# Splitting some stores by rows: 128 rows as 2 and 126, 5 rows as 1 and 4 or 2 and 3

## The chip, the cores and the metric

The kernel runs on one core of one Trainium2 chip. The metric is the device time of one execution in microseconds. A core has the engines PE (matrix products), DVE (vector), ACT (scalar), POOL (general) and SP (here it only issues transfers), and 16 DMA engines that all transfers share. A transfer issued by SP goes to one queue (q1 in the profile), a transfer issued by POOL to another (q0); every DMA engine works on both.

## The reference

The kernel computes one decode step of a transformer block and its gradients, in bf16:

```python
x = A_x                                                # (2, 1, 640)
h  = x + attn(layernorm(x), k_cache, v_cache, wq, wo)  # 32 heads, 4096 keys, head size 128
h2 = h + relu(layernorm(h) @ w1) @ w2                  # w1: 640 x 1728
...
return (h2, *vjp(grad_out))     # gradients of x, k_cache, v_cache, wq, wo, w1, w2
```

The caches have 2 x 32 x 4096 x 128 elements each, 67 MB, and so have their gradients. The gradients of the weights are outer products of two rows per batch element: wq 640 x 4096, wo 4096 x 640, w1 640 x 1728, w2 1728 x 640.

## The kernel before

The order of all work is written out by hand: each stage is a Python generator, and a loop at the end of the function takes a step of one, then of another. There are 64 pairs of batch element and head.

**First pass** (`p1_iter`): for each pair, K and V are loaded as [128, 32 x 128] tiles of 1 MB on SP's queue, K is transposed on PE, and scores, softmax and the products that the gradients need are made.

**Second pass** (`p2_iter`): for each pair V is loaded once more (tile Wt, but for a few that are kept), and the gradients gK and gV, 1 MB each, are made on DVE (L954; gV in part on ACT, L1024) and stored, at first on POOL's queue (L1025, L1040), and from the end of the first pass on SP's (L1004, L1025). POOL also makes the small copies pp (L992) that gV needs.

**Beside the second pass** two more generators run. `fin_gen` makes the weight gradients, out_7 (w2), out_6 (w1), out_5 (wo) and out_4 (wq), by calling `outer_rows`. `gx_gen` and `mlp_out` make the gradient of x (out_1) and the output (out_0) and end in `store_row`.

`outer_rows` (L1070) takes the rows of an output in groups. With `cc` rows to a partition and P = nrow / cc partitions (128 in all calls here), partition p holds rows p*cc to p*cc + cc - 1 of the output. For each group it takes a tile `ot` from the pool "f" (a tile comes back no sooner than 13 steps after it was given back), fills it by products on PE (L1093) and copies on ACT (L1099), and stores it with one transfer on POOL's queue (L1101). For out_7 the last 64 rows are stored apart (L1103). There are 18 stores at L1101: three for out_7, three for out_6, six for out_5, six for out_4, most of them of 0.86 to 1.05 MB.

`store_row` (L699) transposes a column of 640 values into 5 rows of 128, copies them on DVE (L705) into one of two halves of a scratch row, and stores them on SP's queue (L706), 1.2 KB. It runs four times.

What sets the order around the change: SP and POOL each issue their transfers strictly in the order of the program, and an issue that waits holds up all that stands behind it on the same engine. SP's transfers take eight semaphores in turn, and POOL's another eight; an issue waits until the transfer that used its semaphore last, eight places before, has landed. It also waits for the engine that filled the tile. A tile that is stored is filled again only when its store has landed.

Of the kernel before, what the change touches and what calls it, by code (L numbers as in the profile page):

```python
# [15 lines left out]
def kernel(  # L16
# [20 lines left out]
    nc = tc.nc  # L37
# [58 lines left out]
    def pst(shape, dtype, role, name):  # L96

        k = banks[role].pop(0)
        banks[role].append(k)
        return ps.tile(shape, dtype, tag=f"bank{k}", bufs=1, name=name)  # L100
# [11 lines left out]
    def take(tag, shape, name):  # L112
        assert free[tag] > 0, (tag, name)
        free[tag] -= 1
        k = homes[tag].pop(0)
        t = pools[k].tile(shape, BF16, tag=tag_of.get(k, f"big{k}"), bufs=1, name=name)
        home_of[id(t)] = (tag, k, t)
        return t
# [9 lines left out]
    def give(t, to=None):  # L128
        tag, k, _ = home_of.pop(id(t))
        to = to or goes_to(tag)  # L130
        owned[tag] -= 1
        owned[to] += 1
        free[to] += 1
        homes[to].append(k)
        given_at[k] = step[0]

    def rested(tag, n):

        return free[tag] > 0 and (forced[0] or step[0] >= given_at.get(homes[tag][0], -n) + n)
# [557 lines left out]
    nrow = [0]  # L697

    def store_row(col_bf, n, dst):  # L699

        t = pst([16, 128], BF16, "mid", "row_ps")
        nc.tensor.transpose(t[0:n, :], col_bf, ident_bf[:])
        r = junk_row[0:16, D - 128 * (1 + nrow[0] % 2):D - 128 * (nrow[0] % 2)]
        nrow[0] += 1
        nc.vector.tensor_copy(out=r[0:n, :], in_=t[0:n, :])  # L705
        nc.sync.dma_start(out=dst, in_=r[0:n, :])  # L706

    def ttr(in0, in1, acc, width, kc=128, junk=None):
        if junk is None:
# [57 lines left out]
    def mlp_out():  # L767

        ml32 = sm("ml32", FP32, ND, B)
        nc.vector.memset(ml32[:], 0.0)  # L770
        for k in range(NW2):
            while free["q"] < 1 or "arow" not in FIN:
                yield 0.0 if "arow" not in FIN else 0.5
            t = load_w2(k, "q", "(p c) d -> p c d")
            yield from wait(12)
            c1 = min(NF, (k + 1) * FP)
            m_ps = pst([128, ND, B], FP32, "mid", "mlp_ps")
            for c in range(ND):
                for cf in range(k * FP, c1):
                    kc = f_kc(cf)  # L780
                    nc.tensor.matmul(m_ps[:, c, :], lhsT=t[0:kc, cf - k * FP, c * 128:(c + 1) * 128],
                                     rhs=arow[0:kc, cf, :], start=(cf == k * FP), stop=(cf == c1 - 1))
            give(t)
            yield
            nc.vector.tensor_tensor(out=ml32[:], in0=m_ps[:], in1=ml32[:], op=ALU.add)
        ml_bf = sm("ml_bf", BF16, ND, B)
        nc.vector.tensor_copy(out=ml_bf[:], in_=ml32[:])
        y_bf = sm("y_bf", BF16, B, ND)
        nc.vector.tensor_tensor(out=y_bf[:].rearrange("p b c -> p c b"), in0=h1c[:], in1=ml_bf[:], op=ALU.add)
        yield from wait(3)  # L790
        for b in range(B):
            store_row(y_bf[:, b, :], ND, out_0[b].rearrange("s (c p) -> (s c) p", p=128))
            yield
# [272 lines left out]

    late = {}
    spreading = [False]

    def outer_rows(L, nrow, R, N, out_ap, cc, rest=0):  # L1070

        P = nrow // cc
        grp = max(1, min(cc, 4096 // N))
        out_v = out_ap[0:nrow, :].rearrange("(p c) n -> p c n", c=cc)
        for c0 in range(0, cc, grp):
            gn = min(grp, cc - c0)
            while not rested("f", 13):
                yield 0.0
            ot = take("f", [128, grp, N], "ot")
            todo = [(k, n0, min(512, N - n0), P, L[:, bass.ds(c0 + k, P, step=cc)])  # L1080
                    for k in range(gn) for n0 in range(0, N, 512)]
            more = rest if c0 + gn == cc else 0
            assert not more or gn < grp
            if more:
                todo += [(gn, n0, min(512, N - n0), more, L[:, nrow:nrow + more]) for n0 in range(0, N, 512)]
            made = []
            for x in range(len(todo) + 1):
                if x < len(todo):
                    k, n0, nn, kp, cols_of = todo[x]
                    q = 32 * (fw[0] % 4)  # L1090
                    o_ps = pst([128, 512], FP32, "o", "o_ps")
                    fw[0] += 1
                    nc.tensor.matmul(o_ps[0:kp, 0:nn], lhsT=cols_of[q:q + B], rhs=R[q:q + B, n0:n0 + nn],  # L1093
                                     start=True, stop=True)
                    made.append((o_ps, k, n0, nn, kp))
                    yield 0.3
                if x > 0:
                    o_ps, k, n0, nn, kp = made[x - 1]
                    nc.scalar.copy(out=ot[0:kp, k, n0:n0 + nn], in_=o_ps[0:kp, 0:nn])  # L1099
                    yield 0.3  # L1100
            nc.gpsimd.dma_start(out=out_v[:, c0:c0 + gn, :], in_=ot[0:P, 0:gn, :])  # L1101
            if more:
                nc.gpsimd.dma_start(out=out_ap[nrow:nrow + more, :], in_=ot[0:more, gn, :])  # L1103
            give(ot)

    def fin_gen(fin):
# [13 lines left out]
        FIN["arow"] = True  # L1120
        yield
        yield from outer_rows(FIN["ar"], NFF * 128, FIN["gr"], D, out_7, NFF, F_rem)
        yield from rows_of(fin, ghfc, NF, "ghfr", "rX")
        yield from rows_of(fin, x2c, ND, "x2r", "rD")
        yield from outer_rows(FIN["x2r"], D, FIN["ghfr"], Dff, out_6, ND)
        HH = H // 2
        while ("gh1", B - 1) not in done:
            yield
        yield from rows_of(fin, gh1c, ND, "gh1r", "rD")
        for s0 in range(0, H, HH):  # L1130
            yield from rows_of(fin, OFc[:, s0:s0 + HH, :], HH, "OFr", "rX")
            yield from outer_rows(FIN["OFr"], HH * 128, FIN["gh1r"], D, out_5[s0 * 128:(s0 + HH) * 128, :], HH)
# [7 lines left out]
    def gx_gen(fin):  # L1140
# [50 lines left out]
        for b in range(B):  # L1191
            gxo = sm(f"gxo{b}", BF16, ND)
            nc.vector.tensor_copy(out=gxo[:], in_=gx_bf[:, :, b])
            yield from wait(2)
            store_row(gxo[:], ND, out_1[b].rearrange("s (c p) -> (s c) p", p=128))
            yield
# [232 lines left out]
```

## Time and profile before

| | us |
|---|---|
| median of 3 runs | 892.6 (890.12 to 892.91) |
| the profiled execution | 887.9 |
| its span, from the first to the last instruction | 886.1 |

| engine | busy us | share of the span |
|---|---|---|
| PE | 736.0 | 83% |
| DVE | 690.8 | 78% |
| ACT | 478.0 | 54% |
| POOL | 155.8 | 18% |

| transfers | count | KB each | us from issue to landing, median |
|---|---|---|---|
| Kt, Vt, Wt loads on SP's queue | 180 | 1024 | 18.7, 15.1, 16.4 |
| gK, gV stores on SP's queue | 101 | 1024 | 16.7, 15.1 |
| gK, gV stores on POOL's queue | 27 | 1024 | 10.3, 10.4 |
| ot stores on POOL's queue (L1101) | 18 | 160 to 1024 | 10.5 |
| row stores on SP's queue (L706) | 4 | 1.2 | not told |

The profile is of one execution, and times in it are counted from the start of its span. "DMA" in its slices and windows is the mean busy share of the 16 DMA engines, so that 1.00 is all sixteen busy, and 0.06 is one of them. The trace also has a record of each packet that a DMA engine moved, with its queue, start, duration and size, but not with the engine's number, and a record of each update of a semaphore. A transfer has landed when its semaphore has risen by 16.

### The profile page before, as it was taken

How to read it: one execution, taken by the hardware profiler on the slowest of the kernel's cores; microseconds unless marked ns; L12 is line 12 of the kernel's file. 1: busy time of each engine (PE TensorE's matmuls, PEld its weight loads, DVE VectorE, ACT ScalarE, POOL GpSimd, SP SyncE). 2: the span in 40 equal slices, each digit the busy share in tenths (PEclk: the TensorE clock that was granted, in tenths of full speed). 3: DMA queues.
4: the chain of work that ended last, by engine and by line, in shares of the span. 5: the costliest groups of instructions: out<-in, count | busy, mean ns of one | idle time of the engine just before them, and what ended most of it. 6: DMA issues, size and time to landing. Idle time of an engine off the chain costs nothing.

```text
span 886.1 us, 24945 instructions
## 1 busy us (share of the span) xinstructions
PE 736.0 (83%) x10215; PEld 614.3 (69%) x10215; DVE 690.8 (78%) x1309; ACT 478.0 (54%) x1241; POOL 155.8 (18%) x264
## 2 busy tenths in 40 slices
PE   4999899999999998878967777878878896937971
PEld 4888788888888887777856666656757665625640
DVE  2666698877888887777868797678989998799750
ACT  1344343344565655455546777767756555526661
POOL 1344344343210000010011110011010001101200
PEclk9999899999999999999996556555666756556565
DMA  9999999999889999999999999999999999999995
GB/s 377 425 417 417 421 413 420 424 423 416 323 298 392 424 424 426 423 424 426 423 405 415 422 425 425 425 422 412 419 425 414 419 419 427 415 426 421 408 425 229
DMA packets 56115, 361.87 MB, mean 408 GB/s; under 512 B 5712, under 2 KB 11728, under 8 KB 15296
## 3 DMA queue, kind: packets, MB, share of 16 engines
q1 hardware_dynamic: 49096, 317.04, 86.5%
q0 software_dynamic: 6864, 43.22, 11.7%
q8 instruction: 80, 1.31, 0.5%
q14 instruction: 35, 0.29, 0.1%
q10 hardware_dynamic: 40, 0.01, 0.0%
HBM read 211.11 MB, written 149.13 MB: 407 GB/s over the span
## 4 chain that ended last, share of the span: by engine, by line
PE 38%; DMA 21%; DVE 19%; issue 12%; ACT 8%; SPq 0%; POOL 0%; ACTq 0%; POOLq 0%; DVEq 0%
PE t_ps L482 17%; DMA Vt<-in_A_v_cache_dram 10%; PE m_ps L516 9%; DVE gK L954 5%; DVE gV L954 5%; DMA out_dram<-gK 4%; DVE rows L711 4%; DVE pk L523 3%; ACT t_sb L487 3%; PE s_ps L495 3%; PE u_ps L545 3%; DMA out_dram<-ot 2%; ACT gV L1024 2%; DMA wqs<-in_A_wq_dram 2%; PE dp_ps L495 2%
## 5 line engine op out<-in xcount | busy, mean ns | idle before, releaser
L487 ACT COPY t_sb<-t_ps 128x512 f32<-128x512 f32 x479 | 274.2, 587 | 208.7 <-PE t_ps L482 205.4
L495 PEld LDWEIGHTS <-t_sb 128*128 128x128 bf16 x4096 | 177.7, 102 | 57.2 <-ACT t_sb L487 28.8
L482 PE MATMUL t_ps<-ident_f,Wt 128*128 128x128 f32 x832 | 192.6, 381 | 9.0 <-DMA Wt<-in_A_v_cache_dram 8.4
L523 DVE TENSOR_TENSOR pk<-Kt,ep 128x2048 bf16<-128x2048 bf16 x128 | 156.3, 1222 | 39.7 <-ACT ep L570 31.4
L516 PE MATMUL m_ps<-pk,Vt 128*128 128x129 bf16 x2048 | 170.6, 222 | 13.5 <-DMA Vt<-in_A_v_cache_dram 13.5
L482 PEld LDWEIGHTS t_ps<-ident_f,Wt 128*128 128x128 f32 x832 | 134.7, 197 | 38.1 <-issue 30.6
L482 PE MATMUL t_ps<-ident_f,Kt 128*128 128x128 f32 x1024 | 157.0, 286 | 4.1 <-DMA Kt<-in_A_k_cache_dram 3.4
L954 DVE TENSOR_TENSOR gK<-rb,gsp 128x2048 bf16<-128x2048 bf16 x128 | 153.2, 1222 | 8.9 <-DMA out_dram<-gV 7.1
L516 PEld LDWEIGHTS <-Vt 128*128 128x128 bf16 x2048 | 124.5, 98 | 43.5 <-issue 27.7
L954 DVE TENSOR_TENSOR gV<-rb,pp 128x2048 bf16<-128x2048 bf16 (+1 forms) x128 | 143.3, 1140 | 2.7 <-DMA out_dram<-gK 2.6
L482 PEld LDWEIGHTS t_ps<-ident_f,Kt 128*128 128x128 f32 x1024 | 113.5, 145 | 7.8 <-ACT t_sb L487 3.8
L533 POOL COPY pk<-ep 128x16 bf16<-128x16 bf16 x78 | 83.2, 1069 | 155.6 <-ACT ep L570 80.5
L495 PE MATMUL dp_ps<-gom,t_sb 128*128 128x2 bf16 x2048 | 95.3, 168 | 16.9 <-ACT t_sb L487 16.0
L495 PE MATMUL s_ps<-qm,t_sb 128*128 128x2 bf16 x2048 | 87.6, 164 | 1.3 <-DVE t_sb L485 1.3
L1099 ACT CAST ot<-o_ps 128x512 bf16<-128x512 f32 (+3 forms) x152 | 66.8, 493 | 5.1 <-DMA out_dram<-ot 3.0
L992 POOL COPY pp<-P_bf 128x64 bf16<-128x64 bf16 x64 | 30.3, 478 | 163.6 <-DVE gV L954 152.0
L630 ACT CAST wo_t<-m_ps 128x128 bf16<-128x128 f32 x55 | 14.6, 266 | 78.1 <-PE m_ps L516 77.9
L711 DVE CUSTOM_DVE_ANT_0 rows<-wqs,gqr 128x1024 bf16<-128x1024 bf16 x40 | 48.9, 1221 | 9.6 <-DMA wqs<-in_A_wq_dram 9.4
L990 ACT ACTIVATE rb<-dp_ps,rt 128x256 bf16<-128x256 f32 x64 | 30.3, 473 | 44.2 <-PE dp_ps L985 43.3
L711 DVE CUSTOM_DVE_ANT_0 rows<-wo_t,rows 128x640 bf16<-128x640 bf16 x64 | 52.4, 819 | 0.8 <-ACT rows L688 0.4
L1024 ACT ACTIVATE gV<-rb,pa 128x128 bf16<-128x128 bf16 x152 | 46.5, 392 | 6.4 <-DMA out_dram<-gV 6.4
L711 DVE CUSTOM_DVE_ANT_0 rows<-w_t,rows 128x640 bf16<-128x640 bf16 (+2 forms) x53 | 42.3, 799 | 2.9 <-ACT rows L688 2.7
(205 smaller groups left out, 690.3 us busy)
## 6 DMA issues: line engine op xcount, KB each, us to landing
Kt<-in_A_k_cache_dram SPq DMA_DIRECT2D x64, 1024.0 KB, 18.7
Vt<-in_A_v_cache_dram SPq DMA_DIRECT2D x64, 1024.0 KB, 15.1
Wt<-in_A_v_cache_dram SPq DMA_DIRECT2D x52, 1024.0 KB, 16.4
out_dram<-gK SPq DMA_DIRECT2D x51, 1024.0 KB, 16.7
out_dram<-gV SPq DMA_DIRECT2D x50, 1024.0 KB, 15.1
out_dram<-gV POOLq DMA_DIRECT2D x14, 1024.0 KB, 10.4
out_dram<-gK POOLq DMA_DIRECT2D x13, 1024.0 KB, 10.3
out_dram<-ot POOLq DMA_DIRECT2D x6, 960.0 KB, 10.0
```

The costliest lines, as they stand in the source:

```text
L482: nc.tensor.transpose(t_ps[:, j, :], natf[:, 2 * cc:2 * cc + 2, :].rearrange("p c k -> p (c k)"), ident_f[:])
L487: nc.scalar.copy(out=t_sb[:], in_=t_ps[:])
L495: nc.tensor.matmul(dst[:, sc:sc + 2], lhsT=v[:, j, :, par], rhs=vecs[:, par, :], start=(par == 0), stop=(par == 1))
L516: nc.tensor.matmul(r["m"][:, 0:129], lhsT=r["V"][:, sc, :], rhs=r["pk"][sc // HALF][:, sc % HALF, 0:129], start=(sc == 0), stop=(sc == NSC ...
L523: nc.vector.tensor_tensor(out=p["pk"][k][:, :, 0:128].rearrange("p s (a two) -> p s a two", two=2), in0=p["K"][:, sl, :].rearrange("p s (a ...
L533: nc.gpsimd.tensor_copy(out=col, in_=e)
L711: nc.vector.tensor_tensor_reduce(out=junk[0:kc, 0:width], in0=in0, in1=in1, scale=1.0, scalar=0.0, op0=ALU.mult, op1=ALU.add, accum_out=acc)
L954: nc.vector.tensor_tensor(out=pairs_view(dst[:, sl, :]), in0=row.rearrange("p (a two) -> p a two", two=2)[:, None, :, :].to_broadcast([128 ...
L990: nc.scalar.activation(out=rb[:], in_=bank[:, 128:384], func=ACT.Copy, scale=rt[:, b, h:h + 1])
L992: nc.gpsimd.tensor_copy(out=pp[:], in_=P_bf[:, P_slot[(b, h)], :, None].to_broadcast([128, NSC, 2]))
L1024: nc.scalar.activation(out=gV[:, NSC - act + k, :], in_=c["rb"][:, 0:128], func=ACT.Copy, scale=pa[:, k:k + 1])
L1099: nc.scalar.copy(out=ot[0:kp, k, n0:n0 + nn], in_=o_ps[0:kp, 0:nn])
```

## The change

In `store_row` the 5 rows are stored by two transfers on SP's queue instead of one, alternately of 1 and 4 rows and of 2 and 3 rows. In `outer_rows` every third store of 128 rows (the 2nd, 5th, 8th, 11th, 14th and 17th) is made by two transfers on POOL's queue, one of the first 2 partitions and one of the other 126. The same bytes go to the same places, and tiles, products and copies stay as they are.

```diff
@@ store_row
+        cut = 1 + nrow[0] % 2
         nrow[0] += 1
         nc.vector.tensor_copy(out=r[0:n, :], in_=t[0:n, :])
-        nc.sync.dma_start(out=dst, in_=r[0:n, :])
+        for p0, p1 in ((0, cut), (cut, n)):
+            nc.sync.dma_start(out=dst[p0:p1, :], in_=r[p0:p1, :])
...
+    parts = [0]
...
@@ outer_rows
-            nc.gpsimd.dma_start(out=out_v[:, c0:c0 + gn, :], in_=ot[0:P, 0:gn, :])
+            parts[0] += P == 128
+            cuts = (0, 2, P) if P == 128 and parts[0] % 3 == 2 else (0, P)
+            for p0, p1 in zip(cuts, cuts[1:]):
+                nc.gpsimd.dma_start(out=out_v[p0:p1, c0:c0 + gn, :], in_=ot[p0:p1, 0:gn, :])
             if more:
```

## The prediction

> **What bounds the kernel now.** I read the 40 slices of the page first, then the DMA queues, then the last 25 us in windows, then what SP and POOL wait for, and last the trace's records of single DMA packets and of semaphore updates.
>
> ```profile
> DMA  9999999999889999999999999999999999999995
> GB/s 377 425 417 417 421 413 420 424 423 416 323 298 392 424 424 426 423 424 426 423 405 415 422 425 425 425 422 412 419 425 414 419 419 427 415 426 421 408 425 229
> ...
> q1 hardware_dynamic: 49096, 317.04, 86.5%
> q0 software_dynamic: 6864, 43.22, 11.7%
> ```
>
> The sixteen DMA engines are busy from start to end at 405 to 427 GB/s in nearly all slices, while PE, DVE and ACT have 17%, 22% and 46% of the span idle (section 1). The kernel is as long as its DMAs. The last two lines give the price of a byte: 11.7% of 16 engines' 886.1 us are 1658.7 us for 43.22 MB on POOL's queue (q0), that is 38.4 ns for 1,000 bytes on one engine; SP's queue (q1) gives 38.7. A row of 7,680 bytes costs its engine 0.295 us.
>
> The windows of the drain show more (the last three columns are TensorE's clock, the mean busy share of the 16 DMA engines, and GB/s):
>
> ```profile
> 870.00:872.00 2.00, 0.00 (x0) 0.00 (x0) 0.00 (x0) 0.00 (x0) 0.00 (x0) 0.50 1.03 428
> 874.00:876.00 2.00, 0.00 (x0) 0.00 (x0) 0.00 (x0) 0.00 (x0) 0.00 (x0) 0.50 0.59 244
> 877.00:878.00 1.00, 0.00 (x0) 0.00 (x0) 0.00 (x0) 0.00 (x0) 0.00 (x0) 0.50 0.15 61
> 878.00:880.00 2.00, 0.00 (x0) 0.00 (x0) 0.00 (x0) 0.00 (x0) 0.00 (x0) 0.50 0.07 29
> 880.00:882.00 2.00, 0.00 (x0) 0.00 (x0) 0.00 (x0) 0.00 (x0) 0.00 (x0) 0.50 0.06 25
> 882.00:884.00 2.00, 0.00 (x0) 0.00 (x0) 0.00 (x0) 0.00 (x0) 0.00 (x0) 0.50 0.07 29
> ```
>
> A share of 0.06 is one engine of sixteen. Fifteen engines have ended by 877.6 us; one works alone until 884.5, and the span ends 1.6 us behind it. No transfer is late: one engine is 6.9 us late, with a part of every transfer.
>
> SP's waits say the same (waited for, us in total, times, longest):
>
> ```profile
> SPq L1424 <- DMA out_dram<-ot: 16.0, 1, 16.0
> ...
> SPq L1424 <- DMA out_dram<-gK: 2.3, 1, 2.3
> ```
>
> After its last issue SP does nothing but wait for stores to land.
>
> How did that engine fall behind? A DMA of 128 rows adds 1 to its semaphore 16 times, once for each engine. In the semaphore records the last of the 16 comes 0.2 us behind the 15th at 514 us, 1.3 at 560, 3.7 at 703, 6.7 at 861. And which engine is it? The row stores (L706) of 5 rows show 5 packets of 256 bytes each in the packet records: the first two stores have eight at 798.8 to 799.3 and two at 810.2 and 810.3; the third, four at 842.8 to 843.9 and one at 855.8; the fourth, four at 850.0 to 851.2 and one at 860.9. So a row goes to an engine of its own, and the late engine is **one of the five that a 5-row store uses**. Which of the five isn't told.
>
> **The change, part by part.** The order of the built program shows six of the 18 stores of L1101 made in two (the 2nd, 5th, 8th, 11th, 14th, 17th), and the four of L706. PE, ACT and DVE keep their order. No byte is added.
>
> *POOL.* Six more issues of 0.54 us (median of L1101's 18 issues).
>
> ```profile
> 859.76 0.70 POOL L1101 DMA_DIRECT2D out_dram<-ot  x1 [15.36 <-ACT ot L1099]
> 865.79 0.71 POOL L1101 DMA_DIRECT2D out_dram<-ot  x1 [5.32 <-ACT ot L1099]
> 867.75 0.55 POOL L1101 DMA_DIRECT2D out_dram<-ot  x1 [1.25 <-ACT ot L1099]
> ```
>
> The bracket is POOL's idle time ahead of the issue: 5 to 15 us. Behind a split store stands the copy of pp (L992), for which gV on DVE waits; in the waits of DVE behind 556 us there is none for POOL. Taken at 0; without that cover 6 x 0.54 = 3.2 us. The last store (867.75) is whole and 1.25 us behind the ACT copy that releases it, so the 17th's second issue (866.5 to 867.1) ends before it: 0. ACT's first copy into a reused ot now waits for two parts; it waited once in the whole run (3.0 us). If the second part lands a row, 0.3 us, later, that is at most 0.3 us: 0.
>
> *SP.* Four more issues of 0.29 us (L706: 265/286/344 ns). SP's DMAs take eight semaphores in turn, and each waits for the one eight places before. Where two row stores stand near each other, four of the eight are now small, and six large DMAs under way become four: 4 x 1.05 MB at 420 GB/s are 10.0 us of work. The late engine stays the last to finish each of them, so it never runs dry while SP issues the next; other engines may, and they have 6.9 us in hand. 0; if it fails, a queue once empty per place, about 2 us (the wait of 2.0 to 2.6 us that SP shows per lane), so up to 4 us.
>
> *The dealing of the rows.* Here the time is decided. A store of 128 rows puts 8 on each engine. The six split stores carry rows of 7,680 bytes (three), 6,912 (one) and 8,192 (two): one row of each is 46,336 bytes, 1.78 us at 38.4 ns. How 126 rows are dealt no run here shows. Either **(i)** in equal shares on as many engines as divide them, 14 x 9, and the 2 rows on two; or **(ii)** eight to an engine as before, the last with six, and the 2 rows on the first two engines. By (i) fourteen engines get one row more in each split, +1.78 us in all; if the 2 rows fall on the two left out, these get 1 instead of 8: 7 x 1.78 = 12.5 us less. By (ii) two engines get a row more, one gets two less, thirteen the same. For the late engine: -12.5, +1.78 or 0.
>
> [...]
>
> **Sum.** The late engine ends the run. It gets +1.78 us by (i) unless it is left out, +1.78 by (ii) if it is one of the first two, else 0. I take +1.8: without relief (i) always gives that, and (ii) gives it where the late engine is one of the first two. The profiled execution took 887.9 us (span 886.1 and 1.8 around it), so 889.7; the median of the runs is 892.6, 4.7 above it, and the term, a matter of DMA time, is carried over whole: **894.4**.
>
> **Rivals.**
> *The late engine is relieved* (chance 0.29). By (i), with the 2 rows starting at the same engine as the 5-row stores, the left-out two are two of the five among which the late one is. For it: the lag grows slowly, 0.2 to 6.7 us, and the six splits (603.6, 662.3, 723.8, 776.1, 833.8, 865.8 us) would take away 2.1 us each, 14.3 against the other fourteen, so more than all of it. Then the others end the run: 877.6 + 1.8 = 879.4 instead of 884.5, 5.1 us less: 887.5. Not more than 6.9 less (885.7), for the fifteen are busy all the time already. Against it: 2 of 5, times the chance of (i).
> *The 126 rows move badly* (0.22): the other side. [...] Alone a split store is 128 x 0.295 / 16 = 2.4 us of all engines; if it moved at half its rate, the six would cost 14 us, at two thirds 7. I price it at 5: 897.6. It decides from 0.45 us a split (2.7 us, 0.3%). Against it stands the one store that isn't of 128 rows (landing, last column):
>
> ```profile
> out_dram<-ot POOLq DMA_DIRECT2D x1, 160.0 KB, 6.6
> ...
> out_dram<-ot POOLq DMA_DIRECT2D x1, 80.0 KB, 6.4
> ```
>
> The 64-row store (80 KB) lands as fast as the 128-row one beside it, and its packets take 196 ns as theirs do. It is small, though.
> *All 126 rows on one or two engines* (0.03): 126 x 0.295 = 37 us a split on one engine, some 200 us in all. The 5 rows on 5 engines speak against it; outside the range.
> That the split isn't made is excluded by the order of the built program.
>
> **Numbers.** Forecast (0 to +1.8 us) 0.46, relieved 0.29, badly moved 0.22, few engines 0.03. 0.3% (2.7 us) is about what a measurement of this kernel can tell from no change. Of the forecast's 0.46 I put 0.02 past the bound by the uncovered costs on SP and POOL: faster 0.29, same 0.44, slower 0.27. The likeliest case alone spans 892 to 896.5; the range goes to the relieved case with a little of its further end (886.0) and to the badly moved one (898.0).
>
> **What would show it.** Right: in the windows of the drain one engine (0.06) still alone for 6 us or more, the last semaphore update of a store still 6 to 7 us behind the 15th near 860 us. Relieved: the lag shrinks by 2 us at each of the six splits, and the share falls from 0.5 to 0 within 2 us at the end. Badly moved: packets of the split stores, or of SP's queue beside them, longer than 38 ns for 1,000 bytes, and GB/s below 415 in the slices from 600 us. The forecast is wrong if the 2 rows and the 126 don't share engines and the late one has the 2.

## The result, and the profile after

| | before | after |
|---|---|---|
| median of 7 runs, us | 890.12 (888.81 to 892.91) | 897.21 (894.40 to 899.65) |
| profiled execution, us | 887.9 | 897.21 |
| its span, us | 886.1 | 895.4 |
| 7,680-byte packets on POOL's queue, mean ns | 296 | 330 |
| 4,096-byte packets on POOL's queue, mean ns | 161 | 172 |

The changed kernel takes 1.0072 times as long, with an interval of 1.0048 to 1.0097, so it is slower by 6.4 us (4.3 to 8.6); the two medians lie 7.1 us apart. The median of before is now over seven runs and 2.5 us below that of the three in the prediction. The last two rows are from the packet records: 768 packets of the one size and 1,280 of the other, with the same median (291 and 159 ns) in both kernels. The mean rises because some packets take much longer: 65 and 92 of them take over 1.5 times the median, against 13 and 13 before.

I read the page of after as that of before, slices and queues first:

```profile
DMA  9999999999889999999999999999999999999996
GB/s 380 424 418 417 422 412 419 424 424 406 317 310 408 423 424 424 424 426 424 411 370 394 424 424 425 420 407 389 426 425 385 422 425 424 424 399 382 410 403 251
...
q1 hardware_dynamic: 49096, 317.04, 86.3%
q0 software_dynamic: 7152, 43.23, 11.9%
```

The DMA engines are as busy as before, and the same 317 and 43 MB are moved. But 86.3% of 16 engines' 895.4 us are 12,364 us, against 12,264 before, and 11.9% are 1,705, against 1,659. That is 146 us more engine time for the same bytes, or 9.1 us on each of sixteen. The shares are rounded; summed from the packet records it is 135 us, or 8.5 of the 9.3 us by which the span is longer: 3.5 ahead of the first store of `ot` and 5.0 behind it. So nearly all of the loss is transfers that take longer, and not a new wait.

Two places carry this. The first is ahead of the change: the slices 370 and 394 (448 to 492 us; 405 and 415 before). The first store of `ot` comes at 581.6 us instead of 577.0, and nothing that is changed has run until then. The second is the stretch of the 18 stores. Windows of 80 us (the last two columns are the share of the 16 engines and GB/s), first before, then after:

```profile
560.00:640.00 80.00, 66.56 (x617) 52.02 (x617) 65.47 (x125) 56.36 (x146) 6.53 (x17) 0.54 1.01 419
640.00:720.00 80.00, 66.94 (x705) 53.34 (x704) 73.41 (x115) 46.61 (x102) 7.24 (x15) 0.65 1.01 420
720.00:800.00 80.00, 57.47 (x494) 41.99 (x492) 69.40 (x101) 39.35 (x94) 10.20 (x14) 0.54 1.01 422
```

```profile
560.00:640.00 80.00, 65.92 (x607) 52.28 (x606) 63.77 (x125) 54.78 (x146) 7.77 (x20) 0.50 1.01 408
640.00:720.00 80.00, 67.49 (x714) 53.53 (x713) 73.55 (x116) 47.36 (x104) 7.15 (x16) 0.65 1.01 413
720.00:800.00 80.00, 57.74 (x494) 40.24 (x494) 70.51 (x100) 38.99 (x93) 9.58 (x13) 0.54 1.01 417
```

At one and the same share of 1.01 the engines move 408 instead of 419, 413 instead of 420 and 417 instead of 422 GB/s. As time, that is 11/419, 7/420 and 5/422 of 80 us: 2.1, 1.3 and 0.9, together 4.4 us. Full engines that move less are the mark of packets that take longer. The sum is soft, though: the traces below in which no `ot` store is divided by rows (the row stores alone, the division by columns, the kernel before once more) move 417 to 425, 412 to 424 and 420 to 424 GB/s in these windows, so that only the first of the three differences is clear of what one execution differs from another.

The drain of after shows the same more strongly:

```profile
876.00:878.00 2.00, 0.00 (x0) 0.00 (x0) 0.00 (x0) 0.00 (x0) 0.00 (x0) 0.50 1.04 432
880.00:882.00 2.00, 0.00 (x0) 0.00 (x0) 0.00 (x0) 0.00 (x0) 0.00 (x0) 0.50 0.96 340
884.00:886.00 2.00, 0.00 (x0) 0.00 (x0) 0.00 (x0) 0.00 (x0) 0.00 (x0) 0.50 0.99 328
886.00:888.00 2.00, 0.00 (x0) 0.00 (x0) 0.00 (x0) 0.00 (x0) 0.00 (x0) 0.50 0.61 223
890.00:892.00 2.00, 0.00 (x0) 0.00 (x0) 0.00 (x0) 0.00 (x0) 0.00 (x0) 0.50 0.09 39
```

At 884 us all sixteen are busy at 328 GB/s, where before one engine worked alone. Then the last engines end within a few us: from 888 to 890 us about three are left (a share of 0.20), and behind that one or two (0.09). Most of the seven microseconds that fifteen engines had in hand are used up. The semaphore records show when. Of three stores on SP's queue in before that begin to land at 853 to 858 us, fifteen of the 16 updates come within 4.3 us of the first, and the last at 11.1 to 13.7. Of three of after, at 870 to 880 us, thirteen come within 0.8 us, and the others at 3.7 to 5.1, 7.6 to 8.7 and 8.4 to 9.6. So there are now three late engines instead of one, and the other thirteen still lead the last by some 8 us. They lose that lead behind 880 us, where all engines are busy and move 324 to 340 GB/s.

SP's last waits in after (total, times, longest) are shorter ones, for three kinds of stores, instead of one long and one short; together they are 18.8 us, against 18.3 before:

```profile
SPq L1430 <- DMA out_dram<-gV: 7.7, 1, 7.7
...
SPq L1430 <- DMA out_dram<-ot: 7.3, 1, 7.3
...
SPq L1430 <- DMA out_dram<-gK: 3.8, 1, 3.8
```

To see packets without a yardstick that shifts, I compared each packet behind the first store of `ot` with the ordinary time (the median) of its size, added up the excess and divided it by 16 engines: 4.5 us before, 10.6 after. The three other traces without an `ot` store divided by rows have 3.7, 3.9 and 5.9.

### The profile page after: what moved, and what is told of

The parts are those of the page before. It is cut to its first block, busy times and chain, and to the rows that moved or that the text cites. A ratio compares the mean times of both kernels' runs of the same rounds, so it can differ in the third digit from the quotient of the medians.

```text
span 895.4 us, 24958 instructions
## 1 busy us (share of the span) xinstructions
PE 739.5 (83%) x10215; PEld 616.4 (69%) x10215; DVE 691.2 (77%) x1309; ACT 478.4 (53%) x1241; POOL 158.5 (18%) x270
## 3 DMA queue, kind: packets, MB, share of 16 engines
q1 hardware_dynamic: 49096, 317.04, 86.3%
q0 software_dynamic: 7152, 43.23, 11.9%
## 4 chain that ended last, share of the span: by engine, by line
DMA 36%; PE 33%; DVE 13%; ACT 8%; issue 6%; SPq 0%; POOL 0%; ACTq 0%; POOLq 0%; DVEq 0%
PE t_ps L482 16%; DMA Vt<-in_A_v_cache_dram 16%; PE m_ps L516 7%; DMA out_dram<-gK 6%; DMA Wt<-in_A_v_cache_dram 6%; DMA wqs<-in_A_wq_dram 4%; DVE gV L956 3%; ACT gV L1026 3%; DVE gK L956 3%; DVE rows L713 3%; ACT t_sb L487 3%; DVE pk L523 2%; DMA out_dram<-ot 2%; PE s_ps L495 2%; PE u_ps L545 2%
## 5 line engine op out<-in xcount | busy, mean ns | idle before, releaser
L482 PE MATMUL t_ps<-ident_f,Wt 128*128 128x128 f32 x832 | 195.2, 384 | 11.9 <-DMA Wt<-in_A_v_cache_dram 11.3
L482 PEld LDWEIGHTS t_ps<-ident_f,Wt 128*128 128x128 f32 x832 | 136.5, 200 | 41.1 <-issue 34.1
L482 PE MATMUL t_ps<-ident_f,Kt 128*128 128x128 f32 x1024 | 154.7, 283 | 4.7 <-DMA Kt<-in_A_k_cache_dram 3.7
L1107 POOL DMA_DIRECT2D out_dram<-ot x24 | 14.0, 584 | 186.7 <-ACT ot L1102 131.9
## 6 DMA issues: line engine op xcount, KB each, us to landing
Wt<-in_A_v_cache_dram SPq DMA_DIRECT2D x52, 1024.0 KB, 13.5
out_dram<-gV SPq DMA_DIRECT2D x50, 1024.0 KB, 13.5
```

The source lines that it names most:

```text
L482: nc.tensor.transpose(t_ps[:, j, :], natf[:, 2 * cc:2 * cc + 2, :].rearrange("p c k -> p (c k)"), ident_f[:])
```

## The experiments

Two theories stood against each other after the result. By the first, that of **movement** (M in the expectations), a part with fewer than 128 rows makes packets longer, its own and those beside it. By its rival, that of **count or dealing**, the time goes into more transfers, more issues, or an engine that gets more rows. As results came in, the first was taken apart further: is it the shift by two rows (S where the expectations use letters), or the uneven sizes (U), or any division by rows? Every ratio is against the kernel before on the same chip; the runs were made on three chips. Unless it is said otherwise, a kernel keeps all else as before. Where a diff shows only the line of `cuts`, the loop over the parts is that of e2. The labels e1 to e12 are those that the expectations use.

**Only the stores of small rows in two (e1).** The `store_row` part of the change alone.

```diff
+        cut = 1 + nrow[0] % 2
...
-        nc.sync.dma_start(out=dst, in_=r[0:n, :])
+        for p0, p1 in ((0, cut), (cut, n)):
+            nc.sync.dma_start(out=dst[p0:p1, :], in_=r[p0:p1, :])
```

> Only the four row stores on SP's queue are made in two (1 and 4, 2 and 3); the stores of 128 rows stay whole. Theory M (the parts of 126 rows move badly: their packets and their neighbours' are stretched) expects no change, within 1.5 us of before, and one DMA engine alone at the end as before. Theory R (the small parts take four of SP's eight semaphores, so that the other DMA engines run dry near 790 and 840 us) expects most of the 6 to 7 us here. Theory L (the loss stands ahead of any split, at 400 to 500 us, and has another cause) expects a loss there that shows in this kernel or not without regard to the edit.

Measured: 890.92 us, 1.0016 (0.9998 to 1.0033). Up to 2.9 us isn't excluded, but nothing that can be told from no change. Its profiled execution took 897.81, with the first `ot` store only at 585.4 us, and from there to the end of the span 310.6 us (before 309.1). So a delay ahead of the stores comes and goes from one execution to the next, in a kernel without a single divided `ot` store as well.

**Only the six stores as 2 and 126 (e2).**

```diff
+            parts[0] += P == 128
+            cuts = (0, 2, P) if P == 128 and parts[0] % 3 == 2 else (0, P)
+            for p0, p1 in zip(cuts, cuts[1:]):
+                nc.gpsimd.dma_start(out=out_v[p0:p1, c0:c0 + gn, :], in_=ot[p0:p1, 0:gn, :])
```

> Only the six stores of 128 rows are made as 2 and 126; the row stores stay whole. Theory M expects the whole loss, +5 to +7 us, with packets of some split stores 20 to 45% longer than those of whole stores. Theory R expects less than +2. The dealing alone (fourteen engines with one row more in each split) expects +1.8 at most, and the last engine of the drain relieved by up to 12.5 us if it is one of the two left out.

Measured: 894.70 us, 1.0056 (1.0034 to 1.0077), 5.0 us. That is the loss, or nearly all of it. Packet excess behind the first store: 8.0 us. Its drain:

```profile
878.00:880.00 2.00, 0.00 (x0) 0.00 (x0) 0.00 (x0) 0.00 (x0) 0.00 (x0) 0.50 0.99 365
880.00:882.00 2.00, 0.00 (x0) 0.00 (x0) 0.00 (x0) 0.00 (x0) 0.00 (x0) 0.50 0.90 317
```

**The same six stores in two by columns (e3).** As many transfers, issues and bytes as in the run before, but each part has all 128 rows.

```diff
+            parts[0] += 1
+            half = (gn + 1) // 2 if parts[0] % 3 == 2 else gn
+            for k0, k1 in ((0, half), (half, gn)) if half < gn else ((0, gn),):
+                nc.gpsimd.dma_start(out=out_v[:, c0 + k0:c0 + k1, :], in_=ot[0:P, k0:k1, :])
```

> Every third store is made in two as well, but by columns: both parts have all 128 partitions and half of the row's length. As many transfers, issues and semaphores as in e2 (five or six more on POOL's queue), with the rows dealt as before. Theory M expects within 1.5 us of before and no stretched packets of these stores; if the number of transfers is what costs, this is as slow as e2.

Measured: 891.30 us, 1.0008 (0.9985 to 1.0032). Its drain:

```profile
876.00:878.00 2.00, 0.00 (x0) 0.00 (x0) 0.00 (x0) 0.00 (x0) 0.00 (x0) 0.50 1.02 422
880.00:882.00 2.00, 0.00 (x0) 0.00 (x0) 0.00 (x0) 0.00 (x0) 0.00 (x0) 0.50 0.42 174
884.00:886.00 2.00, 0.00 (x0) 0.00 (x0) 0.00 (x0) 0.00 (x0) 0.00 (x0) 0.50 0.06 27
888.00:890.00 2.00, 0.00 (x0) 0.00 (x0) 0.00 (x0) 0.00 (x0) 0.00 (x0) 0.50 0.06 25
```

422/1.02 = 414 GB/s while all are busy, and then one engine alone, as in before. Its packets take 293 and 160 ns in the mean, with none over 2.9 times the median. Packet excess behind the first store: 3.9 us. Six more transfers and six more issues on POOL are free; the count as such falls.

In one thing the two runs differ besides the rows. A half by columns is issued as soon as its own columns are copied, so the halves follow each other by 2.1 to 8.8 us (600.75 and 608.02, for instance), while the parts by rows follow each other by half a microsecond. But the long packets don't need two parts at once. In after, the 2-row part of the store at 608 us has landed at 613.75, and of the 82 packets that the 126-row part still starts behind that, 24 take over 1.5 times the ordinary time; their mean is 450 ns instead of 291.

**All 18 stores as 2 and 126 (e4).**

```diff
+            cuts = (0, 2, P) if P == 128 and gn > 0 else (0, P)
```

> All 18 stores of 128 rows are made as 2 and 126 (row stores whole): three times the dose of e2. Theory M expects about three times the loss of e2, +12 to +20 us. The dealing alone expects +1.8 x 3 = +5.3 at most. If the loss has nothing to do with the splits (theory L), this is as slow as e2.

Measured: 907.62 us, 1.0194 (1.0174 to 1.0214), 17.3 us: three times the dose, 3.5 times the loss. A divided store costs 0.8 us with six and 1.0 us with 18 of them. Its windows:

```profile
720.00:800.00 80.00, 56.52 (x467) 40.08 (x466) 67.45 (x97) 37.30 (x89) 10.68 (x15) 0.50 1.01 397
800.00:880.00 80.00, 62.20 (x527) 42.24 (x526) 58.44 (x81) 49.58 (x106) 11.43 (x18) 0.61 1.01 395
```

```profile
884.00:886.00 2.00, 0.00 (x0) 0.00 (x0) 0.00 (x0) 0.00 (x0) 0.00 (x0) 0.50 1.01 342
890.00:892.00 2.00, 0.00 (x0) 0.00 (x0) 0.00 (x0) 0.00 (x0) 0.00 (x0) 0.50 1.05 281
```

395 to 397 GB/s from engines that are all busy, and 281 at the end. Packets of 356 and 192 ns in the mean; excess 21.0 us. This run also tells how 126 rows are dealt. By (i) of the prediction, 14 engines with nine rows each, 18 splits would leave the two others short of about 37 us of work (126 rows of 0.295 us), and the share would fall well below 1 long before the end; it stays at 0.97 to 1.05 from 870 to 892 us. The packet records show it directly: in after, at 614.8 us, sixteen packets of 7,680 bytes of POOL's queue are under way at one time, all of them begun after the 2-row part had landed (613.75). So all sixteen engines carry rows of the 126, as in (ii). The count of semaphore updates can't tell this, since a part of 2 rows gives 16 as well (580.93 us in this run). Which rows are on which engine isn't shown.

**126 rows first, then 2 (e5).** If the shift by two rows against the dealing of 128 were the cause, this part, which begins at row 0, should be free of it.

```diff
+            cuts = (0, 126, P) if P == 128 and parts[0] % 3 == 2 else (0, P)
```

> The six stores are made as 126 and 2 rows instead of 2 and 126 (row stores whole), so that the large part starts at row 0. Theory S (a start shifted by two rows makes engines read what other engines read) expects the loss to go: within 1.5 us of before. Theory P (dealt in contiguous eights, pairs of engines read from the same part of the SBUF, wherever the part starts) and theory U (126 is not a multiple of 16, whatever follows from that) expect the loss of e2, +3 to +6 us.

Measured: 895.38 us, 1.0048 (1.0026 to 1.0070); packets 341 and 166 ns. The loss stays without the shift, so the shift falls.

**112 and 16 rows (e6).** Both are multiples of 16.

```diff
+            cuts = (0, 112, P) if P == 128 and parts[0] % 3 == 2 else (0, P)
```

> The six stores are made as 112 and 16 rows: both divide evenly over sixteen engines, 7 and 1 rows each, and no engine is loaded more than another. Theory U expects no loss, within 1.5 us. Theory P expects a loss of +2 to +6 us and stretched packets, since seven rows to an engine put engines on one another's rows as well.

Measured: 896.14 us, 1.0058 (1.0031 to 1.0084); packets 318 and 178 ns.

**The kernel before once more (e7)**, for the packets of an unchanged kernel on this chip.

> The kernel before, unchanged, once more: a second trace of it. The first trace of before lost 4 us less between 440 and 490 us, ahead of any split, than the changed kernel's. If that is chance from run to run, this trace may show the longer time there too (as the traces of e1 and e3 did); packets of the stores of 128 rows should again be of normal length, within 6%, and one engine alone at the end of the drain.

Measured: 887.56 us, span 885.8, a single execution; packets 296 and 159 ns, excess 3.7 us; from 878 to 884 us one engine alone (share 0.06 to 0.07). Its first `ot` store came at 577.7 us, so that the early delay did not show in it.

**64 and 64 rows (e8).**

```diff
+            cuts = (0, 64, P) if P == 128 and parts[0] % 3 == 2 else (0, P)
```

> The six stores are made as 64 and 64 rows: even, 4 rows to each engine. Theory U expects no loss, within 1.5 us. Theory P expects the largest loss, +4 to +10 us, if the sixteen engines must read 64 rows through half of the ways that 128 rows have; if rows are free to come by any way, none. The one store of 64 rows that the kernel has already (80 KB) showed packets of normal length, which speaks for none.

Measured: 894.05 us, 1.0033 (1.0009 to 1.0057); packets 332 and 187 ns. With e6, uneven sizes fall too: halves of 64 rows cost and stretch as well. But theory P expected the largest loss here, +4 to +10 us, and got 2.9, the smallest of the divisions in two by rows.

**Only the 17th store (e9)**, the divided one that is nearest to the end, and **only the other five (e10)**.

```diff
+            cuts = (0, 2, P) if parts[0] == 17 else (0, P)
```

> Only the 17th store, the one that moves in the drain, is made as 2 and 126. Theory P (engines that read one another's part of the SBUF) expects +1 to +3 us, with GB/s near 330 at full busy share for some us of the drain; the other stores' packets of normal length. If each split costs the same, +0.8.

Measured: 892.12 us, 1.0019 (1.0002 to 1.0035), 1.7 us.

```diff
+            cuts = (0, 2, P) if parts[0] % 3 == 2 and parts[0] < 17 else (0, P)
```

> The other five splits without the 17th. Theory P expects the rest of the 5 us of e2, +2 to +4, and a drain as in before, with one engine alone for some 6 us. If the loss comes from the drain alone, 0.

Measured: 892.37 us, 1.0031 (1.0014 to 1.0048), 2.8 us. The two add up to 4.5 us, against 5.0 for all six: the loss is neither the drain's alone nor that of the middle alone. The intervals are wide, though: 0.2 to 3.1 us for the one store doesn't exclude the 0.8 of an equal price for each. With the five, one engine is alone at the end for some 3 us and not for the 6 that were expected. The single one in its drain:

```profile
872.00:874.00 2.00, 0.00 (x0) 0.00 (x0) 0.00 (x0) 0.00 (x0) 0.00 (x0) 0.50 1.00 395
874.00:876.00 2.00, 0.00 (x0) 0.00 (x0) 0.00 (x0) 0.00 (x0) 0.00 (x0) 0.50 1.00 356
882.00:884.00 2.00, 0.00 (x0) 0.00 (x0) 0.00 (x0) 0.00 (x0) 0.00 (x0) 0.50 0.06 25
```

All engines busy at 356 GB/s, so the stretch is there; but one engine is still alone at the end, so that the lead of the others may have hidden part of it.

**Four parts of 32 rows (e11), eight parts of 16 rows (e12).**

```diff
+            cuts = tuple(range(0, P + 1, 32)) if parts[0] % 3 == 2 else (0, P)
```

> The six stores are made in four parts of 32 rows, 2 rows to each engine (18 transfers more). [...] If the number of transfers costs, three times that of e8, +9 or more.

Measured: 896.61 us, 1.0083 (1.0054 to 1.0113); packets 335 and 181 ns.

```diff
+            cuts = tuple(range(0, P + 1, 16)) if parts[0] % 3 == 2 else (0, P)
```

> The six stores are made in eight parts of 16 rows, one row to each engine (42 transfers more). [...] If only the number of transfers or their issues cost, in proportion to e8 and e11. If rows are free to come by any way, as e8's or less.

Measured: 900.29 us, 1.0111 (1.0083 to 1.0139); packets 355 and 194 ns. In time, parts of 64, 32 and 16 rows add 6, 18 and 42 transfers and cost 0.33%, 0.83% and 1.11%: not in proportion to the transfers, and those of 32 and 16 rows are not clearly apart. A part of e12's loss has another reason: in its drain POOL waited 4.6 us for parts to land, and issued the last store at 887.0 us only (874.8 in after). Packets of 3.9 times the median and more, of both sizes together, are 58 with parts of 16 rows, 11 with 64, 10 with 32, 12 with 126 first, 17 with 112 and 16, and none in the four traces without an `ot` store divided by rows.

What the runs show together: dividing stores by rows, at each of the rows tried, makes packets longer in some of these stores, and the run with them; dividing as many by columns does neither. The profiled executions say the same without the delay ahead of the first `ot` store: from that store to the end of the span are 308.1 to 311.1 us in the four traces without an `ot` store divided by rows, 312.0 to 315.4 with six divided in up to four parts, 323.6 with eight parts and 324.7 with all 18. Each is one execution, and by this measure e2 (312.4) and the division by columns (311.1) are close; what sets them clearly apart is the median time, 894.7 against 891.3, and the packets.

Why the packets get longer is not shown. The number of rows in a part does not order it by itself: packets of 3.9 times the median and more are 58 with parts of 16 rows, but about as many with 64 rows (11) as with 32 (10); the run with 126 rows first has 12 and that with 112 and 16 rows has 17; and the loss with 64 rows, 2.9 us, was the smallest of the divisions in two by rows, and not the largest. The packet records don't tell the engine, and no run varies the other end of the stores, the DRAM. Theory P of the expectations, by which engines read one another's rows, is so neither shown nor excluded.

## Why the prediction was wrong about the change

Measured were 897.21 us, inside the range of 886 to 898. The likeliest case was a change that can't be told from none; what came was the rival *The 126 rows move badly* (897.6), to which the range had been drawn out. The 2.8 us between 894.4 and 897.21 flatter the forecast, though: its base was the median of three runs, 4.7 us above the profiled execution, and the median of seven lies only 2.2 above it. From there the forecast would have been 890.1 + 1.8 = 891.9, and it was the term for the change that failed: 1.8 us instead of 6.4.

- **What bounds the kernel: right.** The DMA engines do, and the longer packets account for the span. That one engine ends the run was right for before. It held as a cover for a single divided store only in part (1.7 us were paid); with six, three engines are late, and the others lose most of their lead in the drain.
- **POOL at 0: right.**

```profile
866.84 0.72 POOL L1107 DMA_DIRECT2D out_dram<-ot  x1 [17.88 <-ACT ot L1102]
872.85 1.35 POOL L1107 DMA_DIRECT2D out_dram<-ot  x2 [5.29 <-ACT ot L1102]
```

  POOL still stands idle for 5 to 18 us ahead of these issues (the bracket); the two of the 17th store take 1.35 us together and end before the last store is due (874.81). DVE waits for POOL nowhere behind 556 us, and the run by columns, with the same six issues more, shows no loss. ACT waited twice for an `ot` to come free, 1.4 us in all.
- **SP at 0: right within 0.3%.** The row stores alone: 1.0016 (0.9998 to 1.0033); the price of up to 4 us for a queue that runs empty is excluded.
- **The dealing of the rows: the failed step.** Of its two ways, (ii) fits and (i) doesn't, as the run with all 18 stores (a share of 0.97 to 1.05 from 870 to 892 us) and the sixteen packets at 614.8 us show: sixteen engines carry rows of the 126. But the step counted rows alone, 0 to 1.78 us, and took 38.4 ns for 1,000 bytes as fixed. No run shows those 1.78 us; what the runs show in their place is that this price moved: 330 ns for 7,680 bytes are 42.9, in the mean of the six stores with this size, three of them divided. Neighbours on SP's queue stretched as well, if less: of its 8,192-byte packets behind the first `ot` store, 35 take over three times their ordinary 309 ns in after and 70 with all 18 stores divided, against 7 to 13 in the four traces without an `ot` store divided by rows.
- **The late engine is relieved (0.29): did not happen,** since no engine is left out. **All 126 rows on one or two engines (0.03)** is excluded by the same sixteen packets.
- **The 126 rows move badly (0.22): came true,** near its price: the six alone cost 5.0 us (3.0 to 6.9, by the interval of the ratio), and the rival said 5. There is luck in that: the 5 was set below the 7 and 14 of its two workings, with no row behind it. A shift by two rows isn't needed for the loss: 126 rows from row 0 cost 1.0048, those behind the first two 1.0056. Which engine carries which rows no run shows. What spoke against it in the prediction was too weak: the store of 64 rows with packets of 196 ns is one transfer of 80 KB, and here single divided stores also pass without any stretch (1.00 to 1.03 times at 670, 730 and 839 us in after, against 1.45 at 608). One case without a loss says little of a loss that comes in some cases.
- **What would show it:** packets longer than 38 ns for 1,000 bytes and slices below 415 GB/s were named as the marks of this rival. Both are there, but both were set too close to the ordinary: packets of 7,680 bytes take 38.5 ns for 1,000 bytes in before already (42.9 in after), and before itself has slices of 412, 414 and 408 GB/s behind 580 us. What tells the kernels apart is how deep the slices go: 389, 385, 399 and 382 in after.

Open are four things. Why a division by rows makes packets longer, and why some divided stores pass freely; which rows are on which engine then isn't in the records. Why one DMA engine falls behind in before. And what delays some executions by up to 8 us ahead of the first `ot` store, where no kernel differs from before. It comes in different places: in after between 391 and 498 us, while in e1's trace SP's issues are 4 us late at 183 us already and 8 at 436. That speaks for a matter of the execution and not of the kernel, but doesn't show it: the first `ot` store came at 577.0 and 577.7 us in the two traces of before, and at 578.9 to 585.4 in those of the twelve other kernels. The median times speak for a small share in the 6.4 us. The runs by columns and of the row stores had the delay in their profiled executions (581.5 and 585.4 us), and these were 3.1 and 6.9 us slower than the median of their kernels, which are not told apart from before; and the two profiled executions of before were 2.2 and 2.1 us faster than its medians.

None of these versions beats the kernel before.

## What to carry to other kernels

Where the DMA engines bound a kernel, as here, keep a store from the on-chip memory to DRAM at all 128 rows, and if it must be divided, try columns first: six stores in two by columns cost nothing that could be measured, by rows 0.33% to 0.58%. No load was divided here. In such a kernel, put GB/s beside their busy share: a share of 1.0 with falling GB/s (from 720 to 800 us 1.01 at 397 GB/s with all 18 stores divided, against 1.01 at 422 in before) was here a price paid in longer packets, which no count of bytes, rows or instructions finds. And before a term is set at "the same bytes, the same time", look whether the new shape has a row in the trace that is large enough to bear it.

## What the runs showed of the hardware that was not expected

- The price is paid by few packets that take very long. In after 703 of the 768 packets of 7,680 bytes take less than 1.5 times the ordinary 291 ns, and 23 take over 2.5 times, up to 1.4 us; with parts of 16 rows 20 take over four times.
- Long packets also come on the other queue: the excess of all packets behind the first `ot` store, 4.5 us for each engine in before and 10.6 in after, rose from 0.5 to 3.1 on POOL's queue and from 4.0 to 7.5 on SP's, where no large transfer was changed. Part of that may be chance, since SP's queue has 5.6 in the run of the row stores alone; with all 18 stores divided it has 13.5.
- Sixteen busy engines moved as little as 281 GB/s (all 18 stores divided, 890 to 892 us), against 419 to 422 in the windows of before above.
- 126 rows are carried by all sixteen DMA engines, though 126 isn't a multiple of 16 (sixteen packets at one time at 614.8 us in after).
